# A fixed order for the second gate and expert 0's second part, with the indices ahead of the count, the branch behind two output steps and raw loads ahead of the rows

## Chip, cores and metric

The kernel runs on one core of a Trainium2 chip. The metric is device time in microseconds (us), the median of several runs. PE is the matmul engine and PEld its weight load, DVE the vector engine, ACT the scalar engine, POOL and SP the two others; SP issues nearly all transfers, POOL the indirect ones.

## What is computed

Attention over 2 batches of 768 tokens with 8 heads, in which a query sees only the keys of its own bucket of six sign bits; then a mixture of 8 experts with the two best for each token; then one dense layer pair. All in float32.

```python
def _attn_ref(q, k, v, proj):            # q, k, v: 2 x 8 x 768 x 64, proj: 64 x 6
    q_bits, k_bits = (q @ proj > 0), (k @ proj > 0)
    mask = bucket(q_bits)[..., :, None] == bucket(k_bits)[..., None, :]
    scores = np.where(mask, q @ k.T / sqrt(64), -1e9)
    return softmax(scores) @ v
def _moe_ref(x, w_gate, w_noise, noise, w1, w2):   # x: 1536 x 512, w1: 8 x 512 x 1024, w2: 8 x 1024 x 512
    logits = x @ w_gate + log1p(exp(x @ w_noise)) * noise
    top2, top2_w = two best of 8 for each token, softmax of their logits
    out[mask] += top2_w * (relu(x[mask] @ w1[e]) @ w2[e])      # for each expert e
def _moe2_ref(x, w_in, w_out):           # w_in: 512 x 2048, w_out: 2048 x 512
    h = x @ w_in
    return (h - np.tanh(h)) @ w_out
```

## The kernel before

*Stages.* Attention runs first, head by head. Then a gate for each batch chooses two experts per token. Then the eight experts run, and last the dense pair. The change lies where the second batch's gate and expert 0 overlap, in the stretch from about 271 to 345 us of the trace, and a little behind it.

*Segments.* A token's row is written to its expert's place in the DRAM buffer Xg. Expert 0 comes in two segments. n = 0 is its first 128 rows, known from the first batch's gate alone; n = 1 its second part, up to 320 rows (two blocks of 128 and a tail of 64). Segments n = 2 to 8 are experts 1 to 7 with 448 rows each (three blocks and a tail). Each segment goes through eight chunks f of its weights. A hidden step multiplies the rows by the chunk of the first weight (12 matmuls, `h_arm`, L1289, and for n = 0 L1397 inside `seg_fine`); ACT and DVE make of it a high part hh and a low half hl (`h_out`, L1320 and L1322). An output step multiplies these by the chunk of the second weight: 3 matmuls for each block, high by high, high by low, low by high (L1329, L1330, L1331). A tail's output matmuls are L1296. All values are float32, split in two parts for PE. Rows enter by transposing matmuls (`trans_x` L1231, tail `trans_tail` L1247), with the high part copied on ACT and the low half made on DVE (L1233).

*Weights.* `fetch` (L1042, L1044) has SP load a chunk's two raw halves of 256 KB into one of two staging buffers (`wraw`), or for some chunks of expert 0 and 1 into one of three slots in `xT`. `split_w` copies the high part on ACT (L1011) and subtracts for the low half (L1010) on DVE, or on POOL for expert 0 and for expert 1 from its fifth chunk on. In the gate's stretch the low half waits in the list `lows` until it is called for.

*Second gate.* `gate(1)` is a generator that issues on DVE, between PE's steps of segment 0, the noisy logits, the two best, the mask M (L760) and, by matmuls with M on PE (L778 and the like), each token's place in its expert. `mark` and `find` look up which late tokens fall to expert 0, and `gather_x` fetches them with three indirect transfers on POOL (L843). `totals` counts the tokens of each expert (L929 to L934), and `pick_arms` makes from the counts the arm number of each expert (L926): one of four widths of the hidden step, chosen on PE by branches (L1257, L1267). `excess` finds whether some expert has over 448 tokens (cmi, L943). `pick` makes the indices sidx (L853 to L862), by which `scatter` writes the tokens' rows to Xg with twelve indirect transfers on POOL (L866). Only when they have landed can `load_x` read the rows of expert 1 (L1216, L1219, on SP).

*Overflow.* `overflow()` is a branch on all five engines (L1513) on cmi. It isn't taken with these inputs.

*What sets the order.* `seg_fine(0)` yields after each half of a hidden step and after each output step; the table `FILL` says how many of these steps `fill` issues between two pieces of the gate. From here to the overflow branch a scheduler orders PE, DVE and ACT; POOL and SP have the order of the code from `order_p` on. Behind the branch every engine has the order of the code. In the loop of segments, `fetch` runs `PF` = 3 chunks ahead, `load_x(n + 1)` stands behind output step `fx`, and the transposes of the next rows are spread over the last steps.

Of the kernel before, what the change touches and what calls it, by code (L numbers as in the profile page):

```python
# [21 lines left out]
PF = 3  # L22

FILL = (2, 0, 3, 1, 0, 4, 0, 0, 4, 2, 0, 0)
FILL2 = 2
# [30 lines left out]
KEEP = 2  # L56
# [31 lines left out]
def body(tc, q, k, v, proj, w_gate, w_noise, noise, w1, w2, w_in, w_out, out):  # L88
    nc = tc.nc
# [24 lines left out]
    with ExitStack() as ctx:  # L114
# [556 lines left out]
        def gate(b):  # L671
# [133 lines left out]
            if not early:  # L805
                yield from totals()
                yield from excess()
# [7 lines left out]
            for _ in pick(sidx[:, :, b], oh, ts, eng, lead):  # L815
                yield

# [110 lines left out]
        def totals():  # L928
            nc.vector.tensor_copy(tots, gd["tot"])  # L929
            hd["lows"].pop(0)()  # L930
            yield
# [4 lines left out]
        def excess():  # L936
# [3 lines left out]
            yield  # L940
# [3 lines left out]
            yield  # L944
# [398 lines left out]
        def y_out(n):  # L1343
# [8 lines left out]
            for j, ps in enumerate(YP[n][:nb]):  # L1352
                if j % 2:
# [16 lines left out]
        def seg_steps(n, ahead):  # L1370

            YP[n] = y_banks(n)
            for f in range(NF):
                if f + 1 < NF:
                    both_step(n, f + 1)
                else:
                    ahead()
                    tail_step(n, f)
                y_step(n, f)
                yield f  # L1380

        def seg_fine(n):
# [5 lines left out]
            for f in range(NF + 1):  # L1388
                if f < NF:
# [5 lines left out]
                    for dc in range(KD4):  # L1395
                        for w_, x_, st_, sp_ in ((0, xh, dc == 0, False), (0, xl, False, False), (1, xh, False, dc == KD4 - 1)):
                            nc.tensor.matmul(ps[:, :2 * rows].rearrange("p (t n) -> p t n", t=2), ws(t, w_, dc), twice(x_[:, dc]),  # L1397
                                             start=st_, stop=sp_)
                        if dc % 2:
                            yield  # L1400
                    h_out(n, f, ps)
# [77 lines left out]
        gen = gate(B - 1)  # L1479
        next(gen)  # L1480
        fill(FILL[4])
        low0 = find(0)
        next(low0)
        next_w()
        for j, n in enumerate(FILL[5:]):
            next(gen)
            if j == 3:
                next(low0, 0)
            fill(n)
        for _ in gen:  # L1490
            fill(FILL2, KEEP)
# [3 lines left out]
        order_p = ExitStack()  # L1495
        order_p.enter_context(tc.manual_schedule(engines={nc.gpsimd.engine, nc.sync.engine}))
# [3 lines left out]
        run(scatter, B - 1, 0)  # L1500
        run(scatter, B - 1, 1)
        fill(1)
        for dc in range(KD4):
            trans_x(1, dc, "aadd"[dc])
# [177 lines left out]
        def put_out():  # L1682
# [10 lines left out]
        sched = ctx.enter_context(ExitStack())  # L1693
        manual = lambda: sched.enter_context(tc.manual_schedule(engines={nc.tensor.engine, nc.vector.engine, nc.scalar.engine,
                                                                         nc.gpsimd.engine, nc.sync.engine}))
        overflow()
        order_p.close()
        manual()
        while fn[0] < wn[0] + 5:
            fetch()  # L1700
# [4 lines left out]
        hd.pop("lows").pop()()  # L1705
        rest = [gen for gen in (gate_w(B - 1), results())]
# [9 lines left out]
        for n in range(1, NSG):  # L1716
# [8 lines left out]
            fx = 0 if n <= B else 1  # L1725
            if n == B:
                free_gate()
            for f in seg_steps(n, (lambda: h2_step(at(0), None)) if last else (lambda: both_step(n + 1, 0))):
# [105 lines left out]
```

## Time and profile before

| | |
|---|---|
| median of three runs | 882.89 us (881.16, 882.89, 886.14) |
| the profiled execution | 874.63 us, its span 872.9 us |
| PE busy in the span | 855.4 us, 98% |
| DVE, ACT, POOL busy | 667.4, 537.6, 401.4 us |
| granted clock of PE, mean | 0.999 |
| transfers | 127.57 MB, mean 146 GB/s |

The times of the trace are those of one profiled execution, from the start of its span. PE's busy time is a sum over modelled ends of its matmuls; a matmul row's start is when it began, and the distance from one start to the next shows a stall more surely than its end does. The chain of work that ended last goes over PE for 55% of the span and over DVE for 4%.

### The profile page before, as it was taken

What the parts mean: (1) busy time and instruction counts of PE and PEld (TensorE: products, weight loads), DVE (VectorE), ACT (ScalarE), POOL (GpSimd) and SP (SyncE); (2) the same over time, 40 slices, a digit from 0 to 9 for tenths busy, and PEclk for the clock granted to TensorE, in tenths of its full rate; (3) what the DMA queues carried; (4) which work ended last, traced back from release to release, by engine and by line L of the source; (5) the groups of instructions that cost most, each with busy time, mean ns of one, the idle gap of its engine ahead of it and who ended that gap; (6) DMA issues with size and microseconds to landing.
All of it is one profiled execution on the core that took longest, in us unless ns stands there. A gap on an engine that the chain in (4) does not pass through costs nothing.

```text
span 872.9 us, 13694 instructions
## 1 busy us (share of the span) xinstructions
PE 855.4 (98%) x4611; PEld 671.7 (77%) x4611; DVE 667.4 (76%) x1287; ACT 537.6 (62%) x1029; POOL 401.4 (46%) x392
## 2 busy tenths in 40 slices
PE   8999999999999999999999999999999999999998
PEld 3556555555556788788988889898899999999996
DVE  7688778778775655989797979967886676677665
ACT  7667668667455244545444544567787677677665
POOL 6687787898776654210000008522422622632322
PEclk9999999999999999999999999999999999999999
DMA  5646645511134678897977988563300200200001
GB/s 129 147 120 200 212 125 173 159 42 37 50 109 146 228 241 275 235 321 249 305 259 252 303 266 298 193 238 122 93 22 1 89 22 1 85 24 1 25 13 37
DMA packets 112175, 127.57 MB, mean 146 GB/s; under 512 B 33776, under 2 KB 82976, under 8 KB 112080
## 3 DMA queue, kind: packets, MB, share of 16 engines
q1 hardware_dynamic: 105824, 110.38, 40.6%
q0 software_dynamic: 5056, 15.63, 5.3%
q8 instruction: 59, 0.97, 0.5%
q10 hardware_dynamic: 1200, 0.30, 0.2%
q14 instruction: 36, 0.29, 0.1%
HBM read 82.81 MB, written 41.18 MB: 142 GB/s over the span
## 4 chain that ended last, share of the span: by engine, by line
PE 55%; DVE 4%; ACT 2%; issue 1%; POOL 0%; DVEq 0%; POOLq 0%
PE bank L1289 12%; PE bank L1331 9%; PE bank L1329 9%; PE bank L1330 9%; PE bank L1240 4%; PE bank L1238 4%; PE bank L1239 4%; PE bank L1296 2%; PE bank L1231 1%; DVE wt L1010 1%; DVE g_u L1637 1%; PE bank L1606 1%; DVE g_u L1649 0%; ACT hh L1650 0%; DVE hh L1655 0%
## 5 line engine op out<-in xcount | busy, mean ns | idle before, releaser
L1329 PE MATMUL bank<-wt,hh 128*128 128x512 f32 x384 | 152.5, 397 | 2.9 <-PEq L1267 1.2
L1331 PE MATMUL bank<-wt,hh 128*128 128x512 f32 x384 | 152.3, 397 | 0.4 <-DVE hh L1322 0.2
L1630 POOL TENSOR_TENSOR g_th<-g_h,g_th 128x384 f32<-128x384 f32 x64 | 67.0, 1047 | 183.3 <-ACT g_th L1629 182.6
L1330 PE MATMUL bank<-wt,hh 128*128 128x512 f32 x384 | 150.8, 393 | 0.0
L1289 PE MATMUL bank<-xh,wt 128*128 128x400 f32 (+3 forms) x512 | 139.4, 336 | 1.0 <-PEq L1513 1.0
L480 ACT ACTIVATE p<-bank 128x384 f32<-128x384 f32 x192 | 91.8, 488 | 67.2 <-PE bank L479 55.5
L445 DVE TENSOR_REDUCE mx<-bank 128x1 f32<-128x384 f32 x192 | 103.3, 552 | 36.5 <-PE bank L444 34.3
L1010 POOL TENSOR_TENSOR wt<-wraw,wt 128x512 fp32r<-128x512 f32 x34 | 53.6, 1597 | 147.7 <-DMA W2f<-cv_w 133.7
L1289 PEld LDWEIGHTS bank<-xh,wt 128*128 128x128 f32 x512 | 92.8, 189 | 2.7 <-issue 1.1
L1011 ACT ACTIVATE wt<-wraw 128x1024 fp32r<-128x1024 f32 x75 | 79.0, 1055 | 20.2 <-PE bank L1331 17.1
L1240 PE MATMUL bank<-xh,wt 128*128 128x384 f32 x256 | 86.5, 338 | 0.0
L1331 PEld LDWEIGHTS bank<-wt,hh 128*128 128x128 f32 x384 | 72.1, 188 | 18.7 <-DVE hh L1655 1.8
L1238 PE MATMUL bank<-xh,wt 128*128 128x384 f32 x256 | 86.3, 337 | 0.0
L1329 PEld LDWEIGHTS bank<-wt,hh 128*128 128x128 f32 x384 | 72.3, 188 | 18.0 <-issue 2.8
L1239 PE MATMUL bank<-xl,wt 128*128 128x384 f32 x256 | 86.1, 336 | 0.0
L1289 PE MATMUL bank<-xl,wt 128*128 128x400 f32 (+3 forms) x256 | 84.9, 332 | 1.0 <-DVE xl L1233 1.0
L513 POOL TENSOR_TENSOR ps<-ps,p 128x768 f32<-128x768 f32 x45 | 82.3, 1829 | 7.3 <-ACT p L480 2.7
L1320 ACT ACTIVATE hh<-bank 128x448 fp32r<-128x448 f32 (+2 forms) x72 | 36.2, 502 | 79.9 <-issue 27.0
L504 PE MATMUL bank<-p,v 128*64 128x384 f32 x384 | 83.2, 512 | 0.0
L1330 PEld LDWEIGHTS bank<-wt,hh 128*128 128x128 f32 x384 | 72.3, 188 | 12.6
L478 PE MATMUL bank<-qc,kb 108*128 108x384 f32 (+1 forms) x192 | 78.9, 411 | 1.1 <-DVE qc L468 0.9
L1010 DVE TENSOR_TENSOR wt<-wraw,wt 128x1024 fp32r<-128x1024 f32 (+1 forms) x62 | 72.1, 1165 | 4.4 <-ACT wt L1011 4.2
(323 smaller groups left out, 1822.9 us busy)
## 6 DMA issues: line engine op xcount, KB each, us to landing
wraw<-in_moe_w_dram SPq DMA_DIRECT2D x118, 256.0 KB
cv_t<-in_moe_w_in_dram SPq DMA_DIRECT2D x16, 512.0 KB
cv_t<-in_moe_w_out_dram SPq DMA_DIRECT2D x16, 512.0 KB
W2f<-cv_w SPq DMA_DIRECT2D x16, 512.0 KB
wraw<-W2f SPq DMA_DIRECT2D x16, 512.0 KB
Xg<-zero SPq DMA_DIRECT2D x14, 512.0 KB
xy<-Xg SPq DMA_DIRECT2D x7, 768.0 KB
Y<-xy SPq DMA_DIRECT2D x7, 768.0 KB
```

The source lines that it names most:

```text
L445: nc.vector.tensor_reduce(MX[i % 2][:, c, hf:hf + 1], ps[:, :HF], op=ALU.max, axis=AX.X)
L480: nc.scalar.activation(hd["p", i, kc][:, half(hf)], ps[:, :HF], AF.Exp, scale=float(D) ** -0.5)
L504: nc.tensor.matmul(hd["o", i][hf * D:(hf + 1) * D, :HF], raw["v", g][:, par, kc], hd["p", i, kc][:, half(hf)], start=(kc == 0), stop=(kc = ...
L513: eng.tensor_tensor(t, hd["p", i, 0] if kc == 1 else t, hd["p", i, kc], op=ALU.add)
L1010: low = lambda eng, h: eng.tensor_tensor(t[:, 1, h], r[:, h], t[:, 0, h].bitcast(F32), op=ALU.subtract)
L1238: nc.tensor.matmul(ps[:, :n], ws(0, dc), xh[:, dc, :n], start=(dc == 0), stop=False)
L1239: nc.tensor.matmul(ps[:, :n], ws(0, dc), xl[:, dc, :n], start=False, stop=False)
L1240: nc.tensor.matmul(ps[:, :n], ws(1, dc), xh[:, dc, :n], start=False, stop=(dc == KD4 - 1))
L1289: nc.tensor.matmul(col(ps), t[:, w_, 0, ck(dc)], col(x_[l_][:, dc]), start=(dc == 0 and (w_, l_) == (0, 0)), stop=(dc == KD4 - 1 and w_ == 1))
L1329: nc.tensor.matmul(ps[:m], a, t[:, 0, 1], start=first, stop=False)
L1330: nc.tensor.matmul(ps[:m], a, t[:, 1, 1], start=False, stop=False)
L1331: nc.tensor.matmul(ps[:m], l, t[:, 0, 1], start=False, stop=last)
```

## The change

The second gate, the rest of segment 0 and the start of segment 1 get a fixed order on all five engines.

- The gate's pieces are dealt out anew (`FILL`), `find(0)` begins together with the gate, and the position matmuls with M stand between the two halves of hidden step h4 of segment 0.
- `totals` no longer stops for a weight's low half; it is followed at once by the indices, and `excess` comes behind them. The arms of experts 1 to 7 are picked behind the branch.
- The branch stands behind the last two output steps of segment 0 and the tail's transposes. Before, the scheduler had put one hidden step of segment 1 ahead of it.
- Inside the fixed order the transposes of segment 1 stand ahead of output step y6 of segment 0, and the last hidden tile of segment 0 is taken over one half step earlier in the code. The outputs of segment 0 are copied on ACT.
- In segment 1, `load_x` of expert 1's rows stands in the code behind step 4 rather than 0, raw loads run up to five chunks ahead at steps 2 and 3, and the transposes of columns 2 and 3 of expert 1's rows stand ahead of output step 6 rather than behind it.

```diff
-FILL = (2, 0, 3, 1, 0, 4, 0, 0, 4, 2, 0, 0)
-FILL2 = 2
+FILL = (2, 0, 3, 1, 3, 3, 2, 3, 2)
 ...
             if not early:
-                yield from totals()
-                yield from excess()
+                totals()
             ts = w("g_ts", [128, NC, E])
 ...
             for _ in pick(sidx[:, :, b], oh, ts, eng, lead):
                 yield
+            if not early:
+                yield
+                excess()
 ...
         def totals():
             nc.vector.tensor_copy(tots, gd["tot"])
-            hd["lows"].pop(0)()
-            yield
 ...
             for j, ps in enumerate(YP[n][:nb]):
-                if j % 2:
+                if j % 2 or n == 0:
                     nc.scalar.activation(yo[:m, j], ps[:m], AF.Copy)
 ...
-        def seg_steps(n, ahead):
+        def seg_steps(n, ahead, mid=lambda f: None):
 ...
+                mid(f)
                 y_step(n, f)
 ...
-        gen = gate(B - 1)
+        gen, low0 = gate(B - 1), find(0)
+        next(gen)
+        next(low0)
         next(gen)
         fill(FILL[4])
-        low0 = find(0)
-        next(low0)
+        for _ in range(3):
+            next(gen)
+        fill(FILL[5])
         next_w()
-        for j, n in enumerate(FILL[5:]):
+        next(low0, 0)
+        next(gen)
+        next(gen)
+        fill(FILL[6])
+        for _ in range(3):
             next(gen)
-            if j == 3:
-                next(low0, 0)
-            fill(n)
-        for _ in gen:
-            fill(FILL2, KEEP)
+        fill(FILL[7])
+        hd["lows"].pop(0)()
+        fill(FILL[8])
+        assert next(gen, 1) is not None
         fill(left[0], KEEP)
         load_arm(1)
         start.close()
-        order_p = ExitStack()
-        order_p.enter_context(tc.manual_schedule(engines={nc.gpsimd.engine, nc.sync.engine}))
+        sched = ctx.enter_context(ExitStack())
+        sched.enter_context(tc.manual_schedule(engines={nc.tensor.engine, nc.vector.engine, nc.scalar.engine,
+                                                        nc.gpsimd.engine, nc.sync.engine}))
+        run(scatter, B - 1, 0)
+        run(scatter, B - 1, 1)
+        for dc in range(KD4):
+            trans_x(1, dc, "aadd"[dc])
+        fill(1)
         cnt_ = nc.values_load(cmi[0:1, 0:1], min_val=0, max_val=B * S)
         fetch()
         fetch()
-        run(scatter, B - 1, 0)
-        run(scatter, B - 1, 1)
-        fill(1)
-        for dc in range(KD4):
-            trans_x(1, dc, "aadd"[dc])
         trans_tail(1)
         fill(left[0])
 ...
         overflow()
-        order_p.close()
-        manual()
-        while fn[0] < wn[0] + 5:
-            fetch()
         warm(WARM[4])
         store()
         pick_arms(1, 1, E)
         both_step(1, 0)
         hd.pop("lows").pop()()
+        fetch()
 ...
-            fx = 0 if n <= B else 1
+            fx = 4 if n < B else 0 if n == B else 1
 ...
-            for f in seg_steps(n, (lambda: h2_step(at(0), None)) if last else (lambda: both_step(n + 1, 0))):
+            second = lambda f: [trans_x(B, dc) for dc in (2, 3) if (n, f) == (B - 1, 6)]
+            for f in seg_steps(n, (lambda: h2_step(at(0), None)) if last else (lambda: both_step(n + 1, 0)), second):
                 if not last and f == fx:
                     load_x(n + 1)
 ...
-                while fn[0] < min(wn[0] + (PF if "st" in rings or n < B else 2), len(wsrc)):
+                while fn[0] < min(wn[0] + (5 if n < B and f in (2, 3) else PF if "st" in rings or n < B else 2), len(wsrc)):
                     fetch()
 ...
                 for dc in range(0 if last else KD4):
-                    if f == (5 + dc // 2 if n == B - 1 else 3 + dc):
+                    if f == 3 + dc and n > B - 1 or n == B - 1 and f == 5 and dc < 2:
                         trans_x(n + 1, dc)
```

Three places show what moves. The first is DVE behind the position matmuls: tots and cnt are the counts, arm the arm numbers, exs to cmi the overflow count, g_ts to sidx the indices, hh a hidden tile's low half, wt a weight's low half. Before:

```order
L929 COPY tots<-bank_3677 128x24
L1010 TENSOR_TENSOR wt<-wraw,wt 128x1024
L1322 SCALAR_TENSOR_TENSOR hh<-bank_3278,hh 128x128
L932 TENSOR_TENSOR cnt<-tots 1x8
...
L926 CAST arm<-acc 1x7
L926 CAST arm<-acc 1x1
L937 TENSOR_TENSOR exs<-tots 128x8
...
L943 CAST cmi<-cmx 128x1
L813 SCALAR_TENSOR_TENSOR g_ts<-g_ov_3750,T 128x48
L853 TENSOR_TENSOR g_t_3805<-g_oh_3649,g_ts 128x96
L1322 SCALAR_TENSOR_TENSOR hh<-bank_3276,hh 128x128
L857 TENSOR_REDUCE g_p_3807<-g_t_3805 128x12
L862 CAST sidx<-g_p_3807 128x2x6
```

After, in the same place on DVE:

```order
L930 COPY tots<-bank_3665 128x24
L931 TENSOR_TENSOR cnt<-tots 1x8
L932 TENSOR_TENSOR cnt<-cnt,basev 1x1
L924 TENSOR_SCALAR acc<-cnt 1x1
L926 SCALAR_TENSOR_TENSOR acc<-cnt,acc 1x1 x2
L927 CAST arm<-acc 1x1
L811 SCALAR_TENSOR_TENSOR g_ts<-g_ov_3738,T 128x48
L854 TENSOR_TENSOR g_t_3750<-g_oh_3641,g_ts 128x96
L858 TENSOR_REDUCE g_p_3752<-g_t_3750 128x12
L863 CAST sidx<-g_p_3752 128x2x6
L1319 SCALAR_TENSOR_TENSOR hh<-bank_3276,hh 128x128
L1007 TENSOR_TENSOR wt<-wraw,wt 128x1024
```

The indices now follow the counts at once, with only the one arm number of segment 1 between them; the low halves, the other arms and the overflow count come later.

The second place is PE at the end of segment 0, from the load of the arm number to the first branch. L1329 to L1331 are one output step (y6, then y7), L1231 and L1247 the transposes of segment 1. Before:

```order
L1257 TENSOR_LOAD arm
L1257 ISA x2
L1329 MATMUL bank_3493<-wt,hh 128x512
...
L1331 MATMUL bank_3493<-wt,hh 128x512
L1231 MATMUL bank_3885<-ident,xy 128x128 x2
...
L1231 MATMUL bank_3900<-ident,xy 128x128 x2
L1329 MATMUL bank_3493<-wt,hh 128x512
L1330 MATMUL bank_3493<-wt,hh 128x512
L1247 MATMUL bank_3905<-ident,xy 128x64 x4
L1331 MATMUL bank_3493<-wt,hh 128x512
L1267 COMPARE_AND_BRANCH
L1268 COMPARE_AND_BRANCH
L1289 MATMUL bank_3278<-xh,wt 128x320
```

After, with the load of the overflow count at L1510 and the overflow branch at L1521:

```order
L1254 TENSOR_LOAD arm
L1254 ISA x2
L1228 MATMUL bank_3863<-ident,xy 128x128 x2
...
L1228 MATMUL bank_3878<-ident,xy 128x128 x2
L1326 MATMUL bank_3493<-wt,hh 128x512
L1327 MATMUL bank_3493<-wt,hh 128x512
L1328 MATMUL bank_3493<-wt,hh 128x512
L1510 TENSOR_LOAD cmi
L1244 MATMUL bank_3905<-ident,xy 128x64 x4
L1326 MATMUL bank_3493<-wt,hh 128x512
...
L1328 MATMUL bank_3493<-wt,hh 128x512
L1521 COMPARE_AND_BRANCH
```

The transposes moved from behind y6 to ahead of it, and the overflow branch from behind the first hidden step of segment 1 (L1289) to directly behind y7.

The third place is SP behind the overflow branch: Xg holds the rows of the experts, xy is where expert 1's land, wraw and xT take raw weights. Before:

```order
L1044 DMA wraw<-in_moe_w_dram 128x512
L1359 DMA Y<-xl 128x512
L1216 DMA xy<-Xg 128x1536
L1267 UNCONDITIONAL_BRANCH
L1219 DMA xy<-Xg 128x512
L1267 UNCONDITIONAL_BRANCH
L1042 DMA xT<-in_moe_w_dram 128x4x128
L1044 DMA xT<-in_moe_w_dram 128x512
```

After:

```order
L1356 DMA Y<-xl 128x512
L1264 UNCONDITIONAL_BRANCH
L1039 DMA wraw<-in_moe_w_dram 128x4x128
L1041 DMA wraw<-in_moe_w_dram 128x512
...
L1039 DMA xT<-in_moe_w_dram 128x4x128
L1041 DMA xT<-in_moe_w_dram 128x512
L1264 UNCONDITIONAL_BRANCH
L1039 DMA xT<-in_moe_w_dram 128x4x128
L1041 DMA xT<-in_moe_w_dram 128x512
L1213 DMA xy<-Xg 128x1536
L1264 UNCONDITIONAL_BRANCH
L1216 DMA xy<-Xg 128x512
```

The two pairs of raw weights for xT now stand ahead of the rows' load, not behind it.

## Rows read from the trace of the kernel before

**Rows 1.** The page, part 1: busy time, share of the span, instructions of each engine.

```profile
PE 855.4 (98%) x4611; PEld 671.7 (77%) x4611; DVE 667.4 (76%) x1287; ACT 537.6 (62%) x1029; POOL 401.4 (46%) x392
```

**Rows 2.** Waits of PE, 271:345 us (waited for: us in total, times, longest).

```profile
PE bank L1231 <- DMA xy<-Xg: 1.4, 1, 1.4
PE bank L1289 <- PEq L1513: 1.0, 1, 1.0
PE bank L1329 <- ACT hh L1320: 0.5, 1, 0.5
PE bank L1296 <- DVEq L1513: 0.4, 1, 0.4
PE bank L1331 <- DVE hh L1322: 0.2, 1, 0.2
```

**Rows 3.** Timeline, 282:287 us (start, us, engine line op, [idle before <-releaser]).

```profile
282.04 1.05 ACT L1011 ACTIVATE wt<-wraw 128x1024 fp32r<-128x1024 f32 x1
...
283.28 0.29 DVE L1322 SCALAR_TENSOR_TENSOR hh<-bank,hh 128x128 fp32r<-128x128 f32 x1 [0.66 <-ACT hh L1320]
...
284.09 0.28 PE L1397 MATMUL bank<-xh,wt 128*128 128x256 f32 x1
...
285.52 0.40 PE L1329 MATMUL bank<-wt,hh 128*128 128x512 f32 x1
...
285.80 0.21 DVE L760 TENSOR_TENSOR M<-g_oh 128x48 bf16<-128x48 f32 x1
...
286.68 0.20 PE L778 MATMUL bank<-M,before 128*128 128x48 bf16 x1
```

**Rows 4.** Timeline of DVE and POOL, 290:311 us: counts, gathers, indices, scatters.

```profile
290.11 0.17 DVE L929 COPY tots<-bank 128x24 f32<-128x24 f32 x1
...
292.36 0.14 DVE L932 TENSOR_TENSOR cnt<-tots 1x8 f32<-1x8 f32 x1
...
292.60 0.91 POOL L843 DMA_INDIRECT xy<-Xd,xidx  x1 [0.30 <-issue]
...
295.14 0.17 DVE L862 CAST sidx<-g_p 128x12 int32<-128x12 f32 x1
...
295.77 1.01 POOL L866 DMA_INDIRECT Xg<-x,sidx  x1 [2.26 <-DVE sidx L862]
...
310.41 0.97 POOL L866 DMA_INDIRECT Xg<-x,sidx  x1 [0.30 <-issue]
```

**Rows 5.** Timeline, 293:300 us: arm number, y6, first transposes, branch.

```profile
293.21 0.29 DVE L926 CAST arm<-acc 1x7 int32<-1x7 f32 x2
...
294.46 0.49 PE L1329 MATMUL bank<-wt,hh 128*128 128x512 f32 x1 [0.54 <-ACT hh L1320]
...
295.25 1.04 PE L1231 MATMUL bank<-ident,xy 128*128 128x128 f32 x8
...
299.87 0.37 PE L1289 MATMUL bank<-xh,wt 128*128 128x232 f32 x1 [0.96 <-PEq L1513]
```

**Rows 6.** SP's waits, 270:350 us (first row); then timeline, 310:324 us.

```profile
SPq L1216 <- DMA Xg<-x,sidx: 6.6, 1, 6.6
...
310.66 1.22 DVE L1010 TENSOR_TENSOR wt<-xT,wt 128x1024 fp32r<-128x1024 f32 x1
...
314.32 0.32 SPq L1216 DMA_DIRECT2D xy<-Xg  x1
...
316.89 0.39 PE L1331 MATMUL bank<-wt,hh 128*128 128x512 f32 x1
...
318.73 1.38 PE L1231 MATMUL bank<-ident,xy 128*128 128x128 f32 x8 [1.45 <-DMA xy<-Xg]
...
322.84 1.03 PE L1231 MATMUL bank<-ident,xy 128*128 128x128 f32 x8
```

**Rows 7.** Windows (us, busy and count by engine, PEclk, DMA share, GB/s).

```profile
296.00:304.00 8.00, 6.66 (x46) 5.56 (x45) 5.20 (x15) 3.63 (x9) 6.17 (x7) 1.00 0.95 304
350.00:380.00 30.00, 27.98 (x140) 24.19 (x139) 29.37 (x41) 15.59 (x21) 6.53 (x5) 1.00 0.85 263
```

More of the change, by code (lines that the diff above doesn't have):

```diff
@@ L939, in excess @@
             nc.vector.tensor_scalar(exs, exs, 0.0, None, op0=ALU.max)
-            yield
             cmx = gx.tile([128, 1], F32, name="cmx")
@@ L943, in excess @@
             nc.vector.tensor_copy(cmi, cmx)
-            yield
         def results():
@@ L1398, in seg_fine @@
                                              start=st_, stop=sp_)
+                        if dc + 1 == KD4 and f + 1 == NF:
+                            h_out(n, f, ps)
                         if dc % 2:
                             yield
-                    h_out(n, f, ps)
+                    if f + 1 < NF:
+                        h_out(n, f, ps)
                 if f > 0:
@@ L1690, in body @@
         at = lambda n: steps2[n] if 0 <= n < len(steps2) else None
-        sched = ctx.enter_context(ExitStack())
-        manual = lambda: sched.enter_context(tc.manual_schedule(engines={nc.tensor.engine, nc.vector.engine, nc.scalar.engine,
-                                                                         nc.gpsimd.engine, nc.sync.engine}))
         overflow()
-        order_p.close()
-        manual()
-        while fn[0] < wn[0] + 5:
-            fetch()
         warm(WARM[4])
```

## The prediction

> **What bounds the kernel now.** I read the views in this order: the page, the waits of PE, then the timeline around each wait. The page says that PE is busy for 98% of the span [rows 1], so other engines matter only where PE waits for them. Between 271 and 345 us, the stretch that the change touches, the waits of PE are five single events, 3.5 us in all [rows 2]: 1.4 for the rows of expert 1, 1.0 for its own sequencer at the overflow branch, 0.5 ahead of an output step, 0.4 for DVE behind the same branch, 0.2 for the low half of a hidden tile. Nothing else in these 74 us is to be had. The list counts from modelled matmul ends, so a stall can be some tenths larger than its row. I call the eight hidden steps of expert 0's first part h0 to h7, the output steps y0 to y7, and hA and hB the first two hidden steps of its second part.
>
> **The change part by part.** The sum is made against the profiled execution, 874.63 us (span 872.9, the rest around it). It lies 8.3 us under the median of the three timed runs, 882.89, so a saving is scaled by 882.89/874.63 = 1.01 and taken off the median.
>
> *The mask M and the half steps.* Before, y3 runs from 285.52 to the first position matmul at 286.68, 1.16 us, where y6 takes 0.79, from 294.46 to 295.25 [rows 3, 5]; 0.37 is lost because DVE makes hl of h3 only after the whole gate chain. After, the position matmuls stand in the middle of h4, ahead of y3, and this loss is gone. But now PE reaches them earlier than M does. h4 takes 285.52 - 284.09 = 1.43, its first half ends at 284.80. M is ready at 285.80 + 0.21 = 286.01. It comes earlier after the change: DVE sat 0.66 for ACT's hidden tile, which stood behind a 1.05 us weight split on ACT [rows 3]; the split is now behind two hidden tiles, so M ends near 285.35. PE waits some 0.6 (ends: 0.3 where PE comes late, 1.2 where DVE gains nothing). Net +0.25, between -0.1 and +0.85. It is the one place where the change adds a wait: queued behind it on PE are the second half of h4, y3 and all that follows.
>
> *Arm value.* Ahead of y6 PE loads the arm number of the second part. DVE's cast of it runs from 293.21 to 293.50 and y6 starts at 294.46 after 0.54 idle [rows 5]; the row names ACT, whose tile for y6 had long been made, so the load is what came last. After, the cast stands directly behind the totals. DVE then skips the 2.1 us between tots (290.11 to 290.28) and cnt (292.36) [rows 4], in which it waited for a hidden tile and made a weight's low half, and also the seven other experts' arms, so the value is there some 3 us before PE asks. What is left is the load itself. -0.4, between 0 and -0.54.
>
> *Branch.* Before, the overflow branch stands behind hA and costs PE 1.0 of sequencer time with nothing queued, and DVE reaches it later still, which costs the first tail matmul of hB 0.4 [rows 2, 5]. After, it stands behind y7, with y6, four tail transposes and y7 queued; DVE and ACT go through it ahead of hA. The arm branches of every later step run behind output matmuls of 0.23 each and show no row in the list of waits up to 345 us [rows 2], so a branch behind y7 hides for the most part. I leave 0.3 of the 1.0, since the two value loads and the arm branch of hA stand close to it: -0.7, between 0 and -1.0. The tail matmul's wait goes: -0.4, between 0 and -0.4. The arms of experts 1 to 7, now made on DVE behind the branch, lie beside hA and cost nothing; without that cover they would cost under 0.7, the three instructions and the cast at most 0.15 to 0.3 each as the cast's row has it [rows 5]. The copy of the first part's output goes from DVE to ACT, beside hA as well.
>
> [...]
>
> *Rows of expert 1.* PE stops at 316.89 + 0.23 = 317.1 and goes on at 318.73; the first eight transposes then take 1.38, where the next eight take 1.03 [rows 6]: 1.4 + 0.35 = 1.75 lost. The load of the rows was issued at 314.32, because SP stood 6.6 us for the scatters [rows 6]. The first scatter began at 295.77, 2.26 after the gathers were out, waiting for the indices, which DVE finished at 295.31; the twelve follow each other every 1.33, the last at 310.41 [rows 4]. After, the indices don't wait for the count nor for the 2.1 us above: they end by 291.8, ahead of the gathers' end at 292.60 + 0.91 = 293.5. So the scatters begin between 292.6 (the gathers too are up to 0.9 earlier, as h5 now follows the search for late tokens) and 293.8, the last one at 307.2 to 308.4, and with the 3.9 between the last issue and SP's release before, the rows may be read from 311.1 to 312.3. SP now issues two pairs of raw weights ahead. The second waits for DVE's low half of the buffer that it overwrites, done before at 310.66 + 1.22 = 311.88 [rows 6], now 1.1 earlier by the terms so far (0.25 - 0.4 - 0.7 - 0.4 + 0.15, the last below): 310.8. Two issues of about half a us each, and the row load goes out at 311.8. Before, 4.4 passed from its issue to the first transpose: 316.2. PE is there at 317.1 - 1.1 = 316.0. It waits 0.2, and I take -1.55, between -1.75 and +0.5. From there each us of a later issue is a us of PE. Transposing the last two columns ahead of y6 of the second part rather than behind it moves no wait: none stood there.
>
> *Handovers.* h4 in two pieces and y6 behind the transposes add up to two changes of operand of about 0.1: +0.15, between 0 and 0.3.
>
> **Sum:** 0.25 - 0.4 - 0.7 - 0.4 - 1.55 + 0.15 = -2.65. The profiled execution would be 872.0, the median 882.89 - 2.7 = **880.2 us**. What is late next is DVE: from 350 to 380 it is busy for 29.37 of 30 us and PE idles 2.0 there [rows 7]. That work is queued in the order of PE's steps, so I let it move along.
>
> **The rivals.**
>
> *Rows behind the raw loads.* The raw pair issued just ahead of the rows is 0.52 MB, and this core moved 304 GB/s in a full stretch [rows 7]: 1.7 us. If the rows come after it to the full, PE waits 1.9 instead of 0.2, the sum is -0.95, the time 881.9. Against: before, too, weight pairs were in flight with the rows, if issued behind them, and the 4.4 contain that. [...] Chance 0.17.
>
> *Given back at 350 to 380.* If the conversions that fill DVE there are held by their own transfers and not by PE's steps, PE merely waits longer and the time stays: 882.9. For it: DVE has no slack there [rows 7]. Against: its queue is in the order of steps. Chance 0.13.
>
> *More than the sum.* POOL is released from the scatters 2 to 3 us earlier and splits weights of expert 1 earlier; if that takes work out of DVE's way at 350 to 380, up to the 2.0 idle there go: -4.65, 878.2. Chance 0.13.
>
> *Slower: SP stuck ahead of the rows.* SP takes its queue in order, so the row load can't go before the second raw pair, which waits for a DVE low half; before, nothing but the scatters and a store held it. If that low half is late, all of it is PE's. From an issue at 311.8 + 2.65 = 314.5 the change is slower than before, from about 319 by more than 0.5%: some 887. For it: DVE has gate weights and results between the steps there. Against: 310.66 is measured in that order. Chance 0.07.
>
> **How the numbers follow.** The forecast has 0.50. The range leaves out the far part of the slower case and the tail of the large one: 876.5 to 884.5, from the sum's best end (-0.1 - 0.54 - 1.0 - 0.4 - 1.75 = -3.8) with the 2.0 of the third rival to its bad end (0.85 + 0.5 + 0.3 = +1.65). 0.5% (4.4 us, about what a measurement of this kernel can tell from no change) is beyond the forecast; the three runs before spread over 5 us, so a saving of 2.65 may be read as more than 4.4. Faster 0.28 (most of the large case, a third of the forecast), slower 0.06, the same 0.66.
>
> **What would show it.** In the profile after: a PE wait for M of 0.3 to 1.2 between h4's halves; scatters from 292.6 to 293.8; the row load near 311.8, behind two raw pairs; no PE wait of 1 us at the branch; the first transpose of expert 1's rows within 0.5 of the last output matmul ahead of it. A row load later than 314.5, or idle of PE from 345 to 372 us grown by 2 or more, would make the prediction wrong.

## The result, and the profile after

The changed kernel took **893.03 us** (median of 7 runs, 887.1 to 893.8), the kernel before beside it 883.53 (7 runs): ratio 1.0095, 95% interval 1.0068 to 1.0121. It is slower by 0.95%, where 880.2 us, 0.3% faster, was forecast, and outside the range.

The profiled execution took 893.03 us, its span is 891.3. The page's busy times of the changed kernel, which answer to [rows 1]:

```profile
PE 860.4 (97%) x4611; PEld 675.4 (76%) x4611; DVE 667.6 (75%) x1286; ACT 538.1 (60%) x1030; POOL 401.8 (45%) x392
```

The work is the same; 18 us of span came to it as idle of PE (13) and as matmuls that took longer (5). PE's waits between 271 and 345 us, the list that answers to [rows 2]:

```profile
PE bank L1244 <- issue: 11.5, 1, 11.5
PE bank L1228 <- DMA xy<-Xg: 2.1, 1, 2.1
PE bank L1326 <- ACT hh L1317: 1.5, 1, 1.5
PE bank L1395 <- issue: 0.9, 1, 0.9
PE bank L1286 <- ACTq L1521: 0.7, 1, 0.7
PE bank L777 <- issue: 0.6, 1, 0.6
```

One stall of 11.5 us ahead of the tail's transposes (L1244) is larger than all of [rows 2]. The timeline there (columns as in [rows 3]; `remote` and `issue` stand where the profile names no instruction that ended the idle time):

```profile
298.75 0.28 PE L1395 MATMUL bank<-xh,wt 128*128 128x256 f32 x1
...
300.20 0.40 PE L1328 MATMUL bank<-wt,hh 128*128 128x512 f32 x1
...
309.12 0.28 ACT L1317 ACTIVATE hh<-bank 128x128 fp32r<-128x128 f32 x1 [11.91 <-remote]
309.43 0.29 DVE L1319 SCALAR_TENSOR_TENSOR hh<-bank,hh 128x128 fp32r<-128x128 f32 x1 [11.89 <-issue]
...
311.21 0.38 ACT L1229 ACTIVATE xh<-bank 128x256 fp32r<-128x256 f32 x1 [1.81 <-remote]
311.63 0.42 DVE L1230 TENSOR_TENSOR xl<-bank,xh 128x256 fp32r<-128x256 f32 x1 [1.91 <-issue]
...
312.11 0.69 PE L1244 MATMUL bank<-ident,xy 64*128 64x64 f32 x4 [11.51 <-issue]
```

PE began the last matmul of h7 at 298.75, so it was done at 299.03. ACT, idle since 297.2, took the tile at 309.12. What it waited for is PE's signal that the tile is done, and the signal came 10 us late: the trace has the rise of this semaphore, which only PE's matmuls raise there, at 309.10. On the quiet chip (below) it rises 0.01 us behind the modelled end of the same matmul, at 293.74. PE itself had gone on meanwhile: the transposes, begun at 298.87, were likewise copied only from 311.21. The tail's transposes wait for DVE's half of the first copy, which the list of the changed kernel's third profile (below) names, and so PE stood still:

```profile
PE bank L1244 <- DVE xl L1230: 13.2, 1, 13.2
```

The cost goes on behind it, as the windows show (columns as in [rows 7]):

```profile
284.00:290.00 6.00, 3.05 (x25) 2.33 (x24) 1.67 (x11) 1.29 (x3) 2.87 (x3) 0.85 0.50 193
290.00:297.00 7.00, 7.00 (x67) 6.23 (x66) 5.58 (x27) 0.44 (x3) 3.96 (x4) 0.64 0.32 90
...
301.00:308.00 7.00, 0.00 (x0) 0.00 (x0) 0.00 (x0) 0.00 (x0) 5.22 (x6) 0.81 0.91 332
308.00:321.00 13.00, 8.15 (x37) 7.00 (x38) 5.23 (x16) 4.11 (x10) 2.56 (x3) 0.58 0.28 102
```

PE's granted clock falls to 0.50 of full speed in both places: from 288.25 us, within 1.5 us of idle ahead of y3, to 295.08, and from 305.31, within the 11.5 us, to 318.97. The mean is 0.64 in 290 to 297 us and 0.58 in 308 to 321, with PE wholly busy in the first of these.

### The profile page after: what moved, and what is told of

The parts are those of the page before. It is cut to its first block, busy times and chain, and to the rows that moved or that the text cites. A ratio compares the mean times of both kernels' runs of the same rounds, so it can differ in the third digit from the quotient of the medians.

```text
span 891.3 us, 13694 instructions
## 1 busy us (share of the span) xinstructions
PE 860.4 (97%) x4611; PEld 675.4 (76%) x4611; DVE 667.6 (75%) x1286; ACT 538.1 (60%) x1030; POOL 401.8 (45%) x392
## 4 chain that ended last, share of the span: by engine, by line
PE 53%; DVE 4%; ACT 2%; issue 1%; POOL 0%; DVEq 0%; POOLq 0%
PE bank L1286 12%; PE bank L1328 8%; PE bank L1326 8%; PE bank L1327 8%; PE bank L1237 4%; PE bank L1235 4%; PE bank L1236 4%; PE bank L1293 2%; PE bank L1228 1%; DVE wt L1007 1%; DVE g_u L1645 1%; PE bank L1614 1%; ACT hh L1658 0%; DVE g_u L1657 0%; DVE hh L1663 0%
```

## The experiments

**Both kernels again, unchanged.** The stalls could belong to the new order, or to single executions whatever the kernel.

> The kernel before, unchanged, once more. Theory 1 (the stalls of the changed kernel belong to its order of work): this profile has no PE wait over 1.5 us between 271 and 345 us, as the first one, and the runs show a mean granted clock of 0.999. Theory 2 (the stalls fall on single executions, whatever the kernel): the profile or some of the runs show a stall of several us there and a clock of 0.99 or less; the 8 us between the profiled execution (874.63) and the median of the timed ones (883) would then be such stalls. Ratio 1.000 by definition.

> The changed kernel, unchanged, once more. Theory 1 (its order of work stalls PE): the idle of 11.5 us ahead of the tail's transposes and the 3 us between 284 and 289 us stand in this profile too, mean clock 0.984 to 0.990, 887 to 894 us, ratio 1.007 to 1.012. Theory 2 (single executions): the stalls are missing or elsewhere in this profile, span under 882.

The kernel before took 883.25 us (ratio 1.0002), the changed one 893.86 (1.0113, 1.0083 to 1.0142). Both theories hold in part. The changed kernel stalls in the same place again: 10.4 us ahead of L1244. But the kernel before stalls too. Its waits in the new profile, 271 to 345 us:

```profile
PE bank L1329 <- ACT hh L1320: 8.3, 3, 5.7
PE bank L1289 <- PEq L1513: 1.3, 1, 1.3
```

And the timeline at the longest of them:

```profile
309.53 0.27 PE L1289 MATMUL bank<-xh,wt 128*128 128x232 f32 x1
...
314.98 0.44 ACT L1320 ACTIVATE hh<-bank 128x320 fp32r<-128x320 f32 x1 [6.70 <-remote]
```

A hidden tile, finished by PE at 309.8, reaches ACT at 314.98: the same late signal, 5 us long. The trace on which the prediction rests, 8.3 us below the median, had none of it. Starts of PE's steps in four traces (us; hC and hE are the third and fifth hidden step of segment 1; "quiet chip" is explained below):

| PE's step | before, [rows 2] | changed, quiet chip | before again | changed, first profile |
|---|---|---|---|---|
| h4 | 284.09 | 283.89 | 284.13 | 283.69 |
| y6 | 294.46 | 294.36 | 296.40 | 299.66 |
| y7 | 296.04 | 295.62 | 297.98 | 312.72 |
| hA | 297.41 | 297.32 | 299.35 | 315.12 |
| hB | 299.87 | 301.38 | 302.19 | 317.82 |
| hC | 303.52 | 307.09 | 305.34 | 321.35 |
| hE | 308.96 | 312.73 | 318.19 | 326.79 |
| expert 1's first transpose | 318.73 | 322.01 | 327.73 | 337.19 |
| expert 1's first hidden step | 323.63 | 327.02 | 332.12 | 342.15 |
| span | 872.9 | 875.9 | 881.4 | 891.3 |

The eight first transposes of segment 1 (0.8 us) stand ahead of y6 in the changed kernel and behind it in the kernel before; the tail's four (0.4) stand ahead of y7 and inside it. By the last two columns the changed kernel loses 3.7 us from h4 to y6 (2.9 without the moved transposes), 11.5 from y6 to y7 and 1.3 to hC, wins back 7.4 from hC to hE, where the kernel before has its stall, and loses 1.4 more to expert 1, where its rows come late.

**Is it the indirect transfers?** POOL's scatters run in just that stretch, 295.90 to 311.2 us. Both kernels without the twelve scatters of the second batch:

```diff
-        run(scatter, B - 1, 0)
-        run(scatter, B - 1, 1)
```

> The kernel before without the twelve indirect transfers that write the second batch's rows to Xg (left out, so the experts miss these rows). Theory A (while POOL's indirect transfers run, PE's signal that a tile is done reaches ACT late, and PE then runs dry): the idle of 5.7 us ahead of an output step near 315 us goes, and with it the half clock of 6.8 us behind it; the first scatters, of batch 0, stay, and so does the 2 us idle near 287. Time 872 to 876 us, clock 0.999. Theory B (the late signal comes from the other traffic, raw weights and stores): the idle stays, 880 to 883.

> The changed kernel without the same twelve transfers (left out). Theory A: the 10 to 11.5 us idle ahead of the tail's transposes goes, and the wait of 2 to 3 us for the rows; the idle of 3 us between 284 and 290 us with its half clock stays. Time 873 to 879 us, clock 0.995 or more. Theory B: 10 us of idle stay somewhere before 320 us, 885 us or more. The difference to the kernel before without the transfers is what the change is worth without late signals: -1 by the steps of the prediction other than the rows, +3 to +5 if the mask's place costs what this trace shows.

The kernel before: 876.94 us, ratio 0.9897 (0.9878 to 0.9915) to the whole one at 885.32. The changed one: 881.44, 0.9960 (0.9937 to 0.9984). The long stalls go. In the changed kernel the last hidden tile is taken at once, and the tail's transposes follow y6 (timeline):

```profile
299.00 0.28 PE L1395 MATMUL bank<-xh,wt 128*128 128x256 f32 x1
...
299.32 0.28 ACT L1317 ACTIVATE hh<-bank 128x128 fp32r<-128x128 f32 x1 [1.85 <-PE bank L1395]
...
300.78 0.46 PE L1244 MATMUL bank<-ident,xy 64*128 64x64 f32 x4
```

So the long stalls need these transfers. What stays falls in the time of the first batch's scatters, 280 to 287.5 us. There the hidden tile for y3, finished by PE at 283.10, is taken 5.6 us late, and PE waits 2.9 for it:

```profile
288.72 0.28 ACT L1317 ACTIVATE hh<-bank 128x128 fp32r<-128x128 f32 x1 [6.70 <-remote]
```

The two medians still differ by 4.5 us, over runs that spread by 6 and 9, and the profile of the kernel before without the transfers still has waits of up to 3.0 us: theory A holds for the long stalls and not for all of the loss.

**One part of the change undone at a time.** The mask's matmuls behind y3, and with them the search for late tokens behind h5, twice:

```diff
-FILL = (2, 0, 3, 1, 3, 3, 2, 3, 2)
+FILL = (2, 0, 3, 1, 3, 5, 2, 1, 2)
```

> The changed kernel with one part undone: the position matmuls stand behind output step y3 again and the search for late tokens behind h5, as before; all else as changed. If the mask's wait in the middle of h4 is the start of it all (idle, then half clock, then the later idle of 11.5 us): both stalls go, clock 0.999, 878 to 884 us, ratio 0.995 to 1.000. If the later idle has a cause of its own: only the 3 us of idle between 284 and 289 and what the half clock there cost (6.8 us at half speed, 3.4 us) go, 885 to 889 us, ratio 1.002 to 1.006, and the 11.5 us stay.

> The changed kernel with the mask's position matmuls behind y3 again, a second time. On a chip where the kernel before runs at 874 to 875 us: the mask's place costs what the traces there show, 0.5 us of a wait and little clock, so 0 to 1 us under the changed kernel of the same call. On a chip where it runs at 883: 3 to 4 us under the changed kernel.

890.23 us, 1.0072 (1.0035 to 1.0110), and 893.79, 1.0081 (1.0065 to 1.0098), where the whole change took 893.86 and 894.7. The rest of the stall stayed (6.8 us at a tail matmul, 3.7 ahead of y3): the mask's place is not the start of it, and the 3 to 4 us expected of the second try were 0.9. The transposes behind y6:

```diff
+        fill(1)
         for dc in range(KD4):
             trans_x(1, dc, "aadd"[dc])
-        fill(1)
```

> The changed kernel with one part undone: the four transposes of segment 1 stand behind output step y6 again. If the chain last hidden tile, copies of the transposes, tail transposes is what stalls because the transposes stand directly behind h7: the idle of 11.5 us ahead of the tail's transposes shrinks below 2 us, 880 to 884 us, ratio 0.996 to 1.001. If ACT's late start of the last hidden tile has another cause: the idle stays at 8 to 12 us, now ahead of y7 or the tail, ratio 1.007 to 1.012.

892.26 us, 1.0117 (1.0070 to 1.0164): nothing won, though the 11.5 us are gone from that place in the profile (of its fastest run, 888.9 us). Waits of 4.9 us at the overflow branch (L1521) and 2.1 at a tail matmul stand elsewhere instead (271 to 345 us):

```profile
PE bank L1286 <- PEq L1521: 4.9, 1, 4.9
PE bank L1293 <- DVE hh L1319: 2.1, 1, 2.1
PE bank L1326 <- ACT hh L1317: 1.4, 1, 1.4
```

The first hidden step ahead of the branch, and the rows ahead of the raw weights:

```diff
+        both_step(1, 0)
         overflow()
...
-        both_step(1, 0)
```

> The changed kernel with one part undone: the first hidden step of segment 1 stands ahead of the overflow branch again, as before. Theory A: the idle isn't the branch's; some 8 to 12 us of late signals stay in 295 to 315 us, ratio 1.007 to 1.013. Rival (the branch right behind y7 makes all engines meet while ACT is late): idle there under 4 us, ratio 0.998 to 1.004.

```diff
-        fetch()
...
-            fx = 4 if n < B else 0 if n == B else 1
+            fx = 0 if n <= B else 1
...
-... min(wn[0] + (5 if n < B and f in (2, 3) else PF if "st" in rings or n < B else 2), ...
+... min(wn[0] + (PF if "st" in rings or n < B else 2), ...
```

> The changed kernel with one part undone: the load of expert 1's rows stands ahead of the raw weights again and raw loads run three chunks ahead. Theory A: the big idle stays, the wait for the rows falls from 2 to 3 us to below 1.5: ratio 1.007 to 1.011. Rival (the raw loads issued early are what congests the stretch): idle before 320 us under 5 us, ratio below 1.004.

894.96 us, 1.0099 (1.0073 to 1.0125), and 893.33, 1.0084 (1.0067 to 1.0101). Neither is the stall's cause; with the rows first, the wait for them is gone from the list, and the stall is 13.6 us instead.

**Parts alone, and another chip.** The next kernels ran on a chip on which the kernel before itself took 874.72 us (23 runs), as in the trace before the prediction.

```diff
-                yield from totals()
-                yield from excess()
+                totals()
...
+                excess()
```

> The kernel before with one part of the change alone: the indices stand ahead of the overflow count and with no low half or hidden tile between; PE and ACT keep their order. Theory A (signals from PE come late while the indirect transfers run, wherever the order needs one): the stall stays about as in the kernel before, 5 to 8 us of idle, ratio 0.997 to 1.003. Rival C (the earlier scatters, closer to the end of segment 0, make the stall larger): ratio 1.004 or more.

876.29 us, 1.0015 (1.0005 to 1.0024), for the indices alone. The next kernel has the four edits of the section above together:

> The changed kernel with the order of PE and SP undone in four parts at once (mask matmuls behind y3, transposes behind y6, first hidden step of segment 1 ahead of the branch, rows ahead of raw weights); the fixed order of DVE and ACT with the indices first stays. If the order of PE's steps makes the stall larger: as the kernel before, ratio 0.998 to 1.003. If the order on DVE and ACT does: ratio 1.005 to 1.010.

876.52 us, 1.0015 (1.0002 to 1.0028). Half of the scatters:

```diff
         run(scatter, B - 1, 0)
-        run(scatter, B - 1, 1)
```

> The changed kernel with six of the twelve transfers of batch 1's rows (those of the second chosen expert left out). Theory A with the stall bound to the time in which the transfers run: they end some 7 us earlier, the idle ahead of the tail's transposes falls from 10-11.5 to 3 to 5 us, 884 to 889 us. If the stall needs only that some run: idle of 8 us or more, 890 us or more.

879.07 us, 1.0042 (1.0019 to 1.0065), from 874.4 to 881.4, a spread that no run here explains; the profiled execution is one of the fast ones, 874.7. The scatters behind the branch:

```diff
-        run(scatter, B - 1, 0)
-        run(scatter, B - 1, 1)
...
         overflow()
+        run(scatter, B - 1, 0)
+        run(scatter, B - 1, 1)
```

> The changed kernel with the twelve transfers issued behind the overflow branch. Theory A: the stall moves with them: none at h7 and the tail's transposes, idle of 4 to 10 us among the hidden steps of segment 1, and the rows come later, so PE waits up to 5 us more at their first transposes: 886 to 894 us. If the stall belongs to the place (last hidden tile, transposes, branch): 8 us or more of idle ahead of the tail's transposes stay, 890 us or more.

879.93 us, 1.0064 (1.0047 to 1.0081), with a wait for the rows of 4.9 us. No profile taken on this chip has a late signal, so none of it decides between the theories on them. What goes with them is the chip: late signals stood in every profile taken on four chips (the kernel before at 883.2 to 885.8 us there), and in none on three (874.7 to 876.0), though the same transfers run there. So the transfers are needed and are not enough. I call the latter chips quiet. For the two first profiles no chip is on record; by their traces the kernel before was taken on a quiet one and the changed kernel on one of the others.

**The changed kernel on a quiet chip.**

> The changed kernel, unchanged, a third time, to see whether the late signals are a matter of the chip. On a chip where the kernel before runs at 874 to 875 us: if the change's loss is the late signals alone, this runs at 871 to 876 us, ratio 0.997 to 1.002, mean clock 0.996 or more, no idle of 10 us; if its order stalls by itself, ratio 1.007 or more. On a chip where the kernel before runs at 883: ratio 1.008 to 1.013 again.

> The changed kernel, unchanged, a fourth time. On a chip where the kernel before runs at 874 to 875 us: if the change's loss is the late signals alone, 871 to 876 us, ratio 0.997 to 1.002, mean clock 0.996 or more, no idle of 10 us ahead of the tail's transposes; if its order stalls by itself, ratio 1.007 or more. On a chip where the kernel before runs at 883 to 886: ratio 1.008 to 1.013 again, with that idle.

The third time it met a chip of the other kind: 894.7 us, 1.0093 (1.0078 to 1.0109). The fourth time a quiet one: 877.12 against 876.00, **1.0024** (1.0011 to 1.0038). So most of the 9.5 us is late signals, but without them no gain of 0.3% is left either. Its waits, 271 to 345 us:

```profile
PE bank L1286 <- issue: 2.4, 1, 2.4
PE bank L1228 <- DMA xy<-Xg: 1.0, 1, 1.0
PE bank L1286 <- ACTq L1521: 0.7, 1, 0.7
PE bank L777 <- DVE M L759: 0.3, 1, 0.3
```

The timeline at the longest, from the last matmul of hA to the first of hB:

```profile
298.65 0.28 PE L1286 MATMUL bank<-xh,wt 128*128 128x232 f32 x1
...
301.38 0.56 PE L1286 MATMUL bank<-xh,wt 128*128 128x232 f32 x1 [2.45 <-issue]
```

The instructions of the arm branches' line on PE, 293 to 310 us (count, duration in ns: least, median, most; first and last start):

```profile
L1264 PEldq COMPARE_BRANCH  x4: 208/323/3657, 296.8 to 307.1; - x4
```

And the window behind it:

```profile
301.00:308.00 7.00, 6.62 (x26) 5.95 (x27) 1.44 (x9) 1.93 (x3) 5.47 (x6) 0.54 0.96 344
```

An arm branch of hB, the second hidden step behind the overflow branch, took 3.66 us where others take 0.2 to 0.4; only hA's 1.3 us of matmuls covered it. PE idled 2.45 us, and then the clock was 0.54 of full speed in the mean of 7 us, in which PE began 26 matmuls. In the trace of the kernel before it began 44 in the same window:

```profile
301.00:308.00 7.00, 6.62 (x44) 5.89 (x43) 3.66 (x22) 3.48 (x6) 5.48 (x6) 1.00 0.95 308
```

The kernel with four parts undone, which has its branch behind hA, ran a second time:

> The changed kernel with the order of PE and SP undone in four parts at once (mask matmuls behind y3, transposes behind y6, first hidden step of segment 1 ahead of the branch, rows ahead of raw weights), a second time. On a chip with the late signals (kernel before 883 to 886 us): if PE's order makes the loss larger, ratio 0.998 to 1.003 and no idle over 7 us; if the order on DVE and ACT with the earlier scatters does, ratio 1.005 to 1.010. On a chip without them (874 to 876 us): 1.000 to 1.003 again.

876.3 us against 875.58, 1.0003 (0.9989 to 1.0016). Its two profiles, of the same code, show the same wait once and once not. The waits of PE and the arm branches' line in the first, 876.96 us:

```profile
PE bank L1286 <- issue: 4.2, 1, 4.2
```

```profile
L1264 PEldq COMPARE_BRANCH  x4: 208/399/3704, 296.1 to 308.2; - x4
```

And in the second, 873.74 us:

```profile
PE bank L1286 <- PEq L1521: 1.0, 1, 1.0
```

```profile
L1264 PEldq COMPARE_BRANCH  x6: 208/332/2023, 296.0 to 308.8; - x6
```

The page of the kernel before lists a DMA queue `q8 instruction` with 59 packets of 16 KB, 0.97 MB in all, which I take for PE's code. In the trace of the first, PE's next 16 KB of code come at 300.3 us, behind the branch; in the second, as in the kernel before and with the indices alone, at 295 to 296, ahead of it, and the long arm branch (2.0 us) falls where output matmuls are queued. In the changed kernel's trace they come at 298.7, behind its branch of 295.0. That the long arm branches wait for this code is read from all 20 traces: of the 15 arm branches over 0.6 us, from segment 1 on, each ends 1.1 to 1.7 us after such a 16 KB block has landed, 13 of them 1.34 to 1.44 after (the 3.66 us one 1.41 after 299.63). The changed order, too, ran with its code in time: with half of the scatters left out the block comes at 294.2, ahead of the branch at 294.8, hB's arm branch takes 0.44 us, and PE has no wait there but the 0.7 at the branch. So the kernel's code alone doesn't decide which comes first. In the 11 runs of the changed kernel on this chip the mean clock was never above 0.998; in 27 of 56 runs of the kernel before on quiet chips it was 0.999 or 1 (their medians 874.0 to 874.5 us on the three chips), in the rest below (876.1 to 876.3).

**No overflow branch at all.**

```diff
-        overflow()
```

> The changed kernel without the overflow branch and its body (left out; with these inputs no expert overflows). Theory F (behind the taken branch PE waits for code: 2.4 us at the second hidden step of segment 1, and the idle brings half clock for 6.8 us, some 2 us more): on a chip where the kernel before runs at 874 to 876 us this runs at 871 to 874, ratio 0.995 to 0.999, clock 0.998 or more, no arm branch over 1 us there. Rival (the loss is the place of the mask or the rows' load): ratio 1.000 to 1.004. On a chip where the kernel before runs at 883 to 886: the late signals stay, ratio 1.004 to 1.010.

> The kernel before without the overflow branch and its body (left out). Theory F: it saves the 1.0 of PE's sequencer and the 0.4 of DVE there at most, ratio 0.998 to 1.000, on a chip where the kernel before runs at 874 to 876 us; the rows then come no earlier and PE waits for them longer, so less than 1.4 arrives. Rival (a taken branch costs 3 us or more in any place): ratio 0.996 or less. On a chip where the kernel before runs at 883 to 886: ratio 0.995 to 1.002.

These met a chip with late signals: 892.67 us, 1.0084 (1.0065 to 1.0104), and 883.92, 0.9986 (0.9971 to 1.0001). There the kernel before gains 0.1% without the branch, which its interval doesn't tell from nothing. The changed one stays 0.8% slower, where with the branch it was 0.9 to 1.1% on such chips, and the stall ahead of L1244 stays at 10.1 us. What the branch is worth to the changed kernel on a quiet chip was not measured.

## Why the prediction was wrong

**The basis.** The step that failed first is the sentence that puts the 8.3 us between the profiled execution and the median down to a factor of 1.01. By the second profile of the kernel before they are not spread over the kernel: they are late signals, in the very stretch that the change touches, and the trace at hand had none of them. No term or rival could contain them. On the chips that have them, the changed kernel pays 8.9 to 10.6 us more, 9.5 in the result; the first profile against the second one of the kernel before puts this down to a stall that is 4 to 5 us longer (11.5 from y6 to y7, for the 7.4 from hC to hE), 2.9 ahead of the transposes and 1.4 at the rows.

**The mask and the half steps** (forecast +0.25). On the quiet chip M ends at 285.04 and PE waits 0.3 for it; from h4 to y7 the table gives 11.95 us before and 11.73 after, -0.22. The 11.73 hold the tail's transposes (0.39, from 295.23 to 295.62), which before come later, so like for like it is -0.6, where the mask, the arm value and the handovers together were to give 0.0. The mechanism was right, and half of the wait that was put at 0.6 came. In the first profile the same place costs 2.9, by late signals and half clock (0.50 from 288.25 to 295.08 us).

**The arm value** (-0.4) is within that sum: no wait ahead of y6 is left.

**The branch** (-0.7, and -0.4 for the tail's matmul). Wrong. From y7 to hC the quiet chip's table gives 7.48 us before and 11.47 after, +4.0, or +4.4 without the tail's transposes in the first of these: 0.7 for the wait at the branch itself (put at 0.3), 1.6 more between hA and hB, where the forecast took off the 1.0 that stood there, and 2.1 from hB to hC (5.71 us for 3.65), all of it the lower clock that follows, 0.54 in 301 to 308 us for 1.00 before. The argument that output matmuls would hide it looked at the branch; what waits for most of the time is the arm branch of hB, with 1.3 us of matmuls ahead of it. Its 3.66 us end 1.41 us after a block of code has landed, at 299.63. The bound of 0 was too kind, since this idle of 2.45 us also cost clock. That the overflow isn't taken means that its body isn't run; whether the jump past the body is what made the code late was not measured on a quiet chip.

**The rows** (-1.55). The first steps were right: the first scatter begins at 292.91 and the last at 307.38, as forecast:

```profile
292.91 1.01 POOL L867 DMA_INDIRECT Xg<-x,sidx  x1 [0.30 <-DVE hh L1319]
...
307.38 0.97 POOL L867 DMA_INDIRECT Xg<-x,sidx  x1 [0.31 <-issue]
```

But the rows went out 3.2 us later than before, not 2.5 earlier. SP's longest wait on the quiet chip, 295 to 345 us:

```profile
SPq L1039 <- DVE hh L1319: 12.9, 2, 11.0
```

Its issues and the first transposes of expert 1 in the timeline:

```profile
312.99 0.38 SPq L1039 DMA_DIRECT2D xT<-in_moe_w_dram  x1
...
315.60 0.38 SPq L1039 DMA_DIRECT2D xT<-in_moe_w_dram  x1
...
317.49 0.33 SPq L1213 DMA_DIRECT2D xy<-Xg  x1
...
322.01 1.32 PE L1228 MATMUL bank<-ident,xy 128*128 128x128 f32 x8 [0.96 <-DMA xy<-Xg]
```

This answers to [rows 6]: 317.49 for 314.32, 1.0 of wait for 1.4. SP stood behind raw pairs that wait for DVE, and DVE's queue is in the order of PE's steps, which the branch had put 3.8 us back. This is the mechanism of the slower rival, and its price was small, because PE, late by 3.8 itself, needed the rows later. It is also why an earlier scatter gains nothing in this order: the rows are held by PE's steps and not by the transfers.

**The rivals.** Rows behind the raw loads: from the rows' issue to the first transpose 4.5 us passed, for 4.4 before, so that rival's 1.7 did not come; but the raw pair had begun 1.9 us ahead and may have been through, so how the rows fare right behind one isn't shown. Nothing was given back or gained at 350 to 380 us: from expert 1's first hidden step to expert 2's PE takes 34.95 us before and 34.88 on the quiet chip, and there the window 3.4 us later reads like [rows 7]:

```profile
353.40:383.40 30.00, 27.96 (x140) 24.23 (x140) 28.93 (x40) 15.52 (x22) 5.97 (x5) 1.00 0.84 258
```

On the quiet chip the terms as measured are -0.6, +4.4 and, for the rows, -0.2 (hC to expert 1's first hidden step), +3.6 in all for the forecast -2.65; the profiled execution took 877.69 us, 3.1 above 874.63. The medians there differ by 1.1 us only (the ratio's interval is 1 to 3.3 us), since about half of the executions of the kernel before show a lower clock too, and 2 us more.

**Open** stays why signals come late on some chips, and why the changed order loses more by them. Each of four parts undone alone, and the branch left out, left 0.7 to 1.2%; all four together ran only on quiet chips. No version faster than both kernels was found.

## What to carry to other kernels

Where the one profile lies well below the median of the timed runs, first find out what the median has and the profile has not, by a second profile, before a single stall of the first is priced. A branch isn't hidden by the work ahead of it alone: what counts is also how much is queued ahead of the next branch behind it, until the code has arrived (here 1.3 us of matmuls ahead of a branch of 3.66). An idle of PE is to be priced with the clock that the trace shows behind it: behind 2.45 us here it was 0.54 in 7 us and cost 2.1 us more, behind 2.1 us for the rows in the first profile it stayed at 1.00. And a load that stands behind others on SP goes out when the last of their waits ends (here at 317.49, behind raw pairs that waited up to 11.0 us), so its term follows the engine that those wait for.

## What the runs showed of the hardware

On four of seven chips signals of PE reached ACT late (by 5.2 us in the second profile of the kernel before, 309.8 to 314.98), in the time when POOL's runs of indirect scatters go out; in the first profile it was 10.1 us (299.03 to 309.12) and the scatters ran from 295.90 to 311.2. Without the second batch's twelve, only those in the time of the first batch's six stay (5.6 us). DMA traffic alone doesn't bring them: in the first profile PE is busy for all but 1 of 35 us while the DMA engines are 0.77 busy, and loses 3 of 10 us where they are 0.68 busy and the first batch's scatters run. The windows:

```profile
280.00:290.00 10.00, 7.05 (x59) 6.07 (x56) 5.13 (x39) 3.22 (x7) 5.92 (x6) 0.91 0.68 242
345.00:380.00 35.00, 34.03 (x179) 30.28 (x178) 24.14 (x37) 17.55 (x24) 12.56 (x18) 1.00 0.77 233
```

On those chips the traces also hold fewer signal events: between 280 and 315 us 246 for the kernel before and 227 without its branch, where the one before the prediction has 692, and 173 to 199 for the changed kernel and its variants with all scatters, where the quiet one has 671. Events are missing there even where nothing is late: from 200 to 271 us, with PE at h4 at the same time, these traces have 645 to 652 for 716 to 719, and without the twelve transfers 330 and 344 from 280 to 315. So the missing events mark the chip, and not the stall. Whether a part of the loss is one of the recording is not shown, since no run here tells a recorded execution from one that isn't.

One and the same code differs by 5.5 us at hC with and without the late code (308.14 and 302.63: 3.2 of longer wait, 4.2 for 1.0; the rest is put down to the clock, since behind the 4.2 output matmuls start 0.42 to 0.45 us apart up to 307.38 and 0.23 from 307.67 on), and by 3.2 at the end, since PE then no longer waits for the rows.
